# One weight's clamp moves from VectorE to GpSimd, and a list scheduler's price for leaving TensorE's tiling doubles

## The chip, the cores and the metric

One core of a Trainium2 chip runs the whole program. The time is device microseconds of one execution, taken as the median of several. The engines are called as in the profile: PE is TensorE, PEld its weight load, DVE is VectorE, ACT is ScalarE, POOL is GpSimd, and SP is SyncE, whose queue issues every DMA of this kernel.

## The reference

Attention with a learned relative bias, then a two-layer feed-forward. Cut to what matters:

```python
# q, k, v: 4 batches x 8 heads x 576 positions x 64
scores = q @ k.T / 8 + bias          # bias[h, i, j] from a 32-wide MLP of log distances
attn   = softmax(scores)
x      = concat_heads(attn @ v)      # 2304 x 512
h      = x @ w_in                    # w_in 512 x 2048, float64
g      = h * sigmoid(h)
out    = g @ w_out                   # w_out 2048 x 512, float64
```

## The kernel before, in words

[...] `prepare` (L377) turns a 128 x 512 block of a weight into two float32r halves, high and low, with `narrow` (L349) before it. A block takes these steps in a row, all on one `w` tile, of which there are two: ACT takes the absolute value of the upper words (`abs`, L356); DVE clamps (`clamp`, L360), shifts (`shift`, L364), ORs in bits of the lower words (`low`, L369) and the sign (`sign`, L374); ACT copies the high half (`split_hi`, L387, recorded at the helper's line L270); POOL or DVE subtracts (`split_lo`, L391, recorded at L275). 32 blocks go through it: 16 of w_in and 16 of w_out, in turns, while block 0 of the feed-forward runs. The finished w_in halves are also stored to DRAM for the five later blocks (L666).

Attention goes by visits. `chunk` (L537) multiplies queries and keys (L561, L552, into PSUM), takes the biased maximum on DVE (L568), the exponential on ACT (L575), transposes on PE (L584) and evicts on ACT or DVE (L270, L272). `visit` (L463) ends with `pv` (L483), which multiplies by the values on half-width tiles of PE's array, 128 x 64. The bias is made by `bias_tile` (L311): POOL, DVE or ACT at L326 or L328, PE at L334 on quarter-width tiles, 128 x 32. The feed-forward (`ff_step`, L627) has matmuls at L633 and L656, the gate at L638 and L642, and a high and low split at L270, L272 and L275. Everything else on PE uses the full 128 x 128 array.

The order of every engine's instructions is made beforehand by `Plan.order` (L118), a list scheduler that simulates the engines with prices written by hand. Each operation has a price for each engine that may run it, a due time (`prio`), and the buffers it needs; when an engine comes free it takes the ready operation with the earliest due time. Where two engines may run an operation, the one with the higher price takes it as if it were due later (L154), except that POOL has no such handicap. For PE the due time of an operation is raised by `KEEP` if its tiling is another than the current one, in three classes (`MODES`, L58: `pv` is 1, `bias_mm` is 2, all others 0), and a change costs `CHANGE` in the simulation. These two lines decide it:

```python
    MODES, CHANGE, KEEP = {"pv": 1, "bias_mm": 2}, 0.19, 1.5
                    wait[e] = [(p + self.KEEP * (self.MODES.get(self.kinds[i], 0) != mode), p, i) for p, i in every]
```

Each engine then runs its list in order, with semaphores between the engines.

Of the kernel before, what the change touches and what calls it, by code (L numbers as in the profile page):

```python
# [12 lines left out]
ALU = mybir.AluOpType  # L13
# [20 lines left out]
def f(ap):  # L34
    return ap.bitcast(F32)
# [11 lines left out]
class Plan:  # L47
# [7 lines left out]
    CALM = 24.0  # L55


    MODES, CHANGE, KEEP = {"pv": 1, "bias_mm": 2}, 0.19, 1.5  # L58
    LAG = {"PE": 0.2, "ACT": 0.15, "DVE": 0.13, "POOL": 0.15, "SP": 0.95}

    def __init__(self, caps, banks):
# [154 lines left out]
def attention_moe_kernel(ctx: ExitStack, tc: tile.TileContext, q, k, v, small, w_in, w_out, lut, ident_d, out):  # L216
    nc = tc.nc
    V, A, G, T, SP = nc.vector, nc.scalar, nc.gpsimd, nc.tensor, nc.sync
    ENG = {"PE": T, "ACT": A, "DVE": V, "POOL": G, "SP": SP}
# [27 lines left out]
    def buf(tag, shape, dtype=F32):  # L247
        return Buf(tag, shape, dtype)

    def bank(tag, n):  # L250
        return Buf(tag, banks=n)

    def tl(b):
        if b.banks:
            return psum[:, b.at, :] if b.banks == 1 else psum[:, b.at:b.at + b.banks, :].rearrange("p a n -> p (a n)")
        if b.t is None:
            n = 1
            for x in b.shape[1:]:
                n *= x
            flat = pools[b.tag].tile([128, sizes[b.tag]], b.dtype, tag=b.tag, name=b.tag)  # L260
            b.t = flat[:, 0:n]
            if len(b.shape) == 3:
                b.t = b.t.rearrange("p (a n) -> p a n", a=b.shape[1])
            if len(b.shape) == 4:
                b.t = b.t.rearrange("p (a b n) -> p a b n", a=b.shape[1], b=b.shape[2])
        return b.t

    def copy(e, out, in_):
        if e == "ACT":
            A.activation(out=out, in_=in_, func=AF.Copy)  # L270
        else:
            ENG[e].tensor_copy(out=out, in_=in_)  # L272

    def sub(e, out, in0, in1):
        ENG[e].tensor_tensor(out=out, in0=in0, in1=f(in1), op=ALU.subtract)  # L275

    def op(kind, where, prio, reads=(), writes=(), shy=6.0):
        def add(fn):
            plan.op(kind, where, prio, fn, reads, writes, shy=shy)
            return fn  # L280
        return add

    def load(kind, prio, writes, fn, bytes, reads=(), plain=False):
        plan.op(kind, ("SP", 0.52 if plain else 0.7), prio, fn, reads, writes, bytes)
# [61 lines left out]
            out=bias_at(st // 8, 16 * (st % 8) * (BW + 15), [[BW + 16, 16], None, [1, BW]]), in_=tl(bsb)), 302592, reads=[bsb])  # L346


    def narrow(t0, w, src):  # L349

        d = buf("G", [128, 512, 2], U32)
        load("ld_wide", t0 - 6, [d], lambda e: SP.dma_start(out=tl(d), in_=src.bitcast(U32).rearrange("p (n t) -> p n t", t=2)), 524288)

        @op("abs", ("ACT", 0.67), t0, reads=[d], writes=[w])
        def _(e):
            A.activation(out=tl(w), in_=f(tl(d)[:, :, 1]), func=AF.Abs, scale=65536.0)  # L356

        @op("clamp", ("DVE", 0.5), t0 + 0.1, writes=[w])
        def _(e):
            V.tensor_scalar(out=tl(w), in0=tl(w), scalar1=2.0, scalar2=8053063168.0, op0=ALU.max, op1=ALU.min)  # L360

        @op("shift", ("DVE", 0.56), t0 + 0.2, writes=[w])
        def _(e):
            V.tensor_scalar(out=tl(w).bitcast(U32), in0=tl(w).bitcast(U32), scalar1=4, scalar2=1,  # L364
                            op0=ALU.logical_shift_left, op1=ALU.logical_shift_right)

        @op("low", ("DVE", 0.9), t0 + 0.3, reads=[d], writes=[w])
        def _(e):
            V.scalar_tensor_tensor(out=tl(w).bitcast(U32), in0=tl(d)[:, :, 0], scalar=29, in1=tl(w).bitcast(U32),  # L369
                                   op0=ALU.logical_shift_right, op1=ALU.bitwise_or)  # L370

        @op("sign", ("DVE", 0.8), t0 + 0.4, reads=[d], writes=[w])
        def _(e):
            V.scalar_tensor_tensor(out=tl(w).bitcast(U32), in0=tl(d)[:, :, 1], scalar=0x80000000, in1=tl(w).bitcast(U32),  # L374
                                   op0=ALU.bitwise_and, op1=ALU.bitwise_or)

    def prepare(t0, src):  # L377

        w, wr = buf("w", [128, DM]), buf("G", [128, 2, DM], F32R)
        if wide:  # L380
            narrow(t0, w, src)
        else:
            load("ld_w32", t0 - 6, [w], lambda e: SP.dma_start(out=tl(w), in_=src), 262144)

        @op("split_hi", ("ACT", 0.62), t0 + 0.5, reads=[w], writes=[(wr, 0)])
        def _(e):
            copy(e, tl(wr)[:, 0, :], tl(w))  # L387

        @op("split_lo", {"POOL": 1.36, "DVE": 0.9}, t0 + 1, reads=[w, (wr, 0)], writes=[(wr, 1)])
        def _(e):  # L390
            sub(e, tl(wr)[:, 1, :], tl(w), tl(wr)[:, 0, :])  # L391
        return wr
# [206 lines left out]
    def split_x(blk, t0):  # L599

        xs = []
        for cc in range(NC):
            t = t0 + 0.5 * cc
            xb, xr = buf("xp", [128, TB]), buf("xp", [128, TB])
            xs.append(buf("M", [128, 2, TB], F32R))
            load("ld_x", t - 6, [xb], lambda e, xb=xb, cc=cc: SP.dma_start(out=tl(xb), in_=x_d[blk][:, cc, :]), 196608, reads=[x_b[blk]])
            for a, x in enumerate(HALF):
                load("ld_rec", t - 6.1, [(xr, a)], lambda e, a=a, x=x, xr=xr, cc=cc: SP.dma_start(out=tl(xr)[x], in_=bass.AP(
                    tensor=rec_d.tensor, offset=rec_d.offset + (2 * cc + a) * NBLK * TB + TB * blk, ap=[[0, 64], [1, TB]])),
                    98304, reads=[rec_b[i] for i in range(TB * blk // S, (TB * blk + TB - 1) // S + 1)], plain=True)  # L610

            @op("x_mul", {"DVE": 0.6, "POOL": 1.15}, t - 0.1, reads=[xr], writes=[xb])
            def _(e, xb=xb, xr=xr):
                ENG[e].tensor_tensor(out=tl(xb), in0=tl(xb), in1=tl(xr), op=ALU.mult)

            @op("x_hi", {"DVE": 0.5, "ACT": 0.52}, t, reads=[xb], writes=[(xs[cc], 0)])
            def _(e, xb=xb, cc=cc):
                copy(e, tl(xs[cc])[:, 0, :], tl(xb))

            @op("x_lo", {"POOL": 1.1, "DVE": 0.66}, t + 0.1, reads=[xb, (xs[cc], 0)], writes=[(xs[cc], 1)])  # L620
            def _(e, xb=xb, cc=cc):
                sub(e, tl(xs[cc])[:, 1, :], tl(xb), tl(xs[cc])[:, 0, :])
        return xs
# [35 lines left out]
    def ff_block(blk, t0, step):  # L659
        xs = split_x(blk, t0 - 8)  # L660
        acc = [bank("acc", 1) for _ in range(3)]
        for fi in range(NF):
            t = t0 + step * fi
            if blk == 0:
                wr = prepare(t - 5, w_in[fi])
                load("st_in", t - 1, [win_b[fi]], lambda e, wr=wr, fi=fi: SP.dma_start(out=win_d[fi], in_=f(tl(wr).rearrange("p a n -> p (a n)"))), 524288, reads=[wr])  # L666
                if wo[fi] is None:
                    wo[fi] = prepare(t - 2, w_out[128 * fi:128 * fi + 128, :])
            else:
                wr = buf("G", [128, 2, DM], F32R)  # L670
                load("ld_in", t - 8, [wr], lambda e, wr=wr, fi=fi: SP.dma_start(out=f(tl(wr).rearrange("p a n -> p (a n)")), in_=win_d[fi]), 524288, reads=[win_b[fi]])
            ff_step(blk, fi, xs, wr, acc, t)
        for i in range(3):
            ob = buf("M", [128, DM])
            t = t0 + step * (NF - 1) + 2 * DF + 3
            cuts = [(0, DM)] if blk < NBLK - 1 or i < 2 else [(0, DM // 2), (DM // 2, DM)]
            for x, y in cuts:
                @op("out_ev", {"ACT": 0.18 + (y - x) * 0.00083, "DVE": 0.15 + (y - x) * 0.00104}, t, reads=[acc[i]], writes=[(ob, x)])
                def _(e, i=i, ob=ob, x=x, y=y):
                    if e == "ACT":  # L680
                        A.activation(out=tl(ob)[:, x:y], in_=tl(acc[i])[:, x:y], func=AF.Copy, scale=0.5)
                    else:
                        V.tensor_scalar_mul(out=tl(ob)[:, x:y], in0=tl(acc[i])[:, x:y], scalar1=0.5)

                row = TB * blk + 128 * i
                load("st_out", t + 1, [], lambda e, ob=ob, row=row, x=x, y=y: SP.dma_start(
                    out=out[row:row + 128, x:y], in_=tl(ob)[:, x:y]), 512 * (y - x), reads=[(ob, x)])
# [3 lines left out]
    t = T0  # L691
    for c in range(5):
        for st in range(8 * c, min(8 * c + 8, 36)):
            bias_tile(st, (t - B1 if c else -60) + BD * (st - 8 * c))
        for hp in range(4):
            if c == 0:
                kv[hp], vs[hp], sq[hp] = keys(0, hp, t), values(0, hp, t), sums(t)
            t = visit(0, hp, (c,), kv[hp], vs[hp], sq[hp], t)
# [7 lines left out]
    for some in ((1, 2), (3,)):  # L706
        for hp in range(4):
            biases.clear()
            for b in some:
                pace = PACE[t > t2]  # L710
                kv, vs, sq = keys(b, hp, t), values(b, hp, t), sums(t)
                for chunks in ((0, 1), (2, 3, 4)):
                    t = visit(b, hp, chunks, kv, vs, sq, t, pace)
# [74 lines left out]
```

## Time and profile before

| | |
|---|---|
| time, median of 3 runs | 736.17 us (735.53 to 736.71) |
| the profiled execution | 736.04 us, of which the span of instructions is 734.3 us |
| PE, DVE, ACT, POOL busy | 97%, 57%, 53%, 38% of the span |
| granted TensorE clock, mean | 0.998 |

The program passes through three stages. In the first some 115 us the bias is made and batch 0's attention runs. From there to about 340 us the attention of the other batches, the preparing of the weights and block 0 of the feed-forward are mixed. After that the feed-forward takes over, alone from about 470 us. Busy times are read by stage, since the averages over the span mix them.

### The profile page before, as it was taken

What the parts mean: (1) busy time and instruction counts of PE and PEld (TensorE: products, weight loads), DVE (VectorE), ACT (ScalarE), POOL (GpSimd) and SP (SyncE); (2) the same over time, 40 slices, a digit from 0 to 9 for tenths busy, and PEclk for the clock granted to TensorE, in tenths of its full rate; (3) what the DMA queues carried; (4) which work ended last, traced back from release to release, by engine and by line L of the source; (5) the groups of instructions that cost most, each with busy time, mean ns of one, the idle gap of its engine ahead of it and who ended that gap; (6) DMA issues with size and microseconds to landing.
All of it is one profiled execution on the core that took longest, in us unless ns stands there. A gap on an engine that the chain in (4) does not pass through costs nothing.

```text
span 734.3 us, 13019 instructions
## 1 busy us (share of the span) xinstructions
PE 712.6 (97%) x4642; PEld 590.1 (80%) x4642; DVE 421.0 (57%) x862; ACT 389.4 (53%) x820; POOL 281.4 (38%) x277
## 2 busy tenths in 40 slices
PE   9899999999999999989999999999999999999997
PEld 4376698677777787778888888899998999999996
DVE  6999968999999999996553544213211221211111
ACT  8899968886786777765443454222222232222222
POOL 5464524474746445573122251123223322422221
PEclk9999999999999999999999999999999999999999
DMA  6998899898584594879856567736454644346001
GB/s 195 372 315 270 277 310 359 278 289 297 191 290 157 203 303 149 272 257 311 293 165 224 168 217 241 263 115 196 148 162 153 186 150 152 125 136 195 1 0 44
DMA packets 68384, 154.77 MB, mean 211 GB/s; under 512 B 9056, under 2 KB 24032, under 8 KB 68320
## 3 DMA queue, kind: packets, MB, share of 16 engines
q1 hardware_dynamic: 68320, 153.94, 63.7%
q8 instruction: 37, 0.61, 0.4%
q14 instruction: 27, 0.22, 0.1%
HBM read 125.12 MB, written 28.79 MB: 210 GB/s over the span
## 4 chain that ended last, share of the span: by engine, by line
PE 46%; issue 7%; DVE 3%; POOL 2%; DMA 1%; ACT 0%; POOLq 0%; DVEq 0%; ACTq 0%
PE psum L633 18%; PE psum L656 18%; PE psum L483 3%; PE psum L561 3%; PE psum L584 3%; POOL M L275 2%; DVE G L568 1%; DVE w L369 1%; DMA G<-in_k_dram 1%; PE psum L552 1%; DVE M L275 0%; DVE w L374 0%; DVE th L642 0%; DVE M L272 0%; DVE w L360 0%
## 5 line engine op out<-in xcount | busy, mean ns | idle before, releaser
L633 PE MATMUL psum<-M,G 128*128 128x384 f32 x1152 | 238.8, 339 | 1.0 <-POOL M L275 0.8
L656 PE MATMUL psum<-G,M 128*128 128x512 f32 x864 | 238.0, 397 | 1.2 <-DVE M L275 0.9
L633 PEld LDWEIGHTS psum<-M,G 128*128 128x128 f32 x1152 | 203.4, 188 | 16.6 <-POOL M L275 1.0
L275 POOL TENSOR_TENSOR M<-th,M 128x384 fp32r<-128x384 f32 x82 | 84.9, 1035 | 272.0 <-ACT M L270 189.3
L642 DVE SCALAR_TENSOR_TENSOR th<-th,psum 128x384 f32<-128x384 f32 x96 | 53.0, 552 | 216.4 <-ACT th L638 216.4
L656 PEld LDWEIGHTS psum<-G,M 128*128 128x128 f32 x864 | 156.7, 188 | 22.2 <-DVE M L275 1.6
L575 ACT ACTIVATE G<-G,sm 128x576 f32<-128x576 f32 (+1 forms) x144 | 111.8, 777 | 53.6 <-DVE sm L568 52.3
L638 ACT ACTIVATE th<-psum 128x384 f32<-128x384 f32 x96 | 47.1, 491 | 161.1 <-PE psum L633 160.0
L568 DVE CUSTOM_DVE_ANT_0 G<-psum,G 128x576 f32<-128x576 f32 (+1 forms) x144 | 106.5, 758 | 27.9 <-PE psum L561 15.5
L584 PE MATMUL psum<-ident,G 128*128 128x128 f32 x656 | 93.5, 276 | 5.7 <-DVE sm L568 3.3
L561 PE MATMUL psum<-G,M 128*128 128x288 f32 x512 | 90.9, 310 | 4.9 <-DVE sm L568 3.5
L584 PEld LDWEIGHTS psum<-ident,G 128*128 128x128 f32 x656 | 75.3, 141 | 23.0 <-issue 4.8
L561 PEld LDWEIGHTS psum<-G,M 128*128 128x128 f32 x512 | 73.9, 190 | 19.7 <-issue 6.7
L483 PE MATMUL psum<-pt,M 128*64 128x128 f32 (+3 forms) x880 | 87.5, 346 | 1.6 <-DVE sm L568 0.8
L483 PEld LDWEIGHTS psum<-pt,M 128*64 128x64 f32 x880 | 52.1, 137 | 30.7 <-issue 6.8
L270 ACT ACTIVATE pt<-psum 128x512 f32<-128x512 f32 (+3 forms) x111 | 59.4, 551 | 28.1 <-PE psum L584 27.0
L275 POOL TENSOR_TENSOR M<-M 64x256 fp32r<-64x256 f32 (+3 forms) x40 | 48.6, 1217 | 57.9 <-DVE M L272 21.0
L270 ACT ACTIVATE M<-th 128x384 fp32r<-128x384 f32 x81 | 42.3, 523 | 40.9 <-DVE th L642 40.0
L272 DVE COPY pt<-psum 128x512 f32<-128x512 f32 (+3 forms) x81 | 45.4, 571 | 21.8 <-PE psum L584 19.1
L275 POOL TENSOR_TENSOR G<-w,G 128x512 fp32r<-128x512 f32 x25 | 35.6, 1425 | 23.8 <-ACT G L270 19.9
L275 POOL TENSOR_TENSOR G<-G 128x576 fp32r<-128x576 f32 x21 | 32.2, 1540 | 29.6 <-PE psum L334 9.6
L326 ACT ACTIVATE G<-lut_sb,cb 128x528 f32<-128x528 f32 (+16 forms) x71 | 41.6, 662 | 0.0
(55 smaller groups left out, 574.1 us busy)
## 6 DMA issues: line engine op xcount, KB each, us to landing
G<-win_d SPq DMA_DIRECT2D x80, 512.0 KB
G<-bias_d SPq DMA_DIRECT2D x48, 576.0 KB
bias_d<-G SPq DMA_DIRECT2D x36, 295.5 KB
G<-in_k_dram SPq DMA_DIRECT2D x16, 576.0 KB
G<-in_w_in_dram SPq DMA_DIRECT2D x16, 512.0 KB
G<-in_w_out_dram SPq DMA_DIRECT2D x16, 512.0 KB
win_d<-G SPq DMA_DIRECT2D x16, 512.0 KB
M<-in_v_dram SPq DMA_DIRECT2D x16, 320.0 KB
```

What stands on the lines that cost most here:

```text
L270: A.activation(out=out, in_=in_, func=AF.Copy)
L272: ENG[e].tensor_copy(out=out, in_=in_)
L275: ENG[e].tensor_tensor(out=out, in0=in0, in1=f(in1), op=ALU.subtract)
L483: T.matmul(out=tl(o)[x, 0:w], lhsT=tl(vs)[:, (s + 1) % 5 * 128 + 64 * a:(s + 1) % 5 * 128 + 64 * a + 64], rhs=tl(pt)[:, s + 5 * a if s < 4 ...
L561: T.matmul(out=s[:, hf, 0:288], lhsT=tl(qs)[:, x0 + 128 * a:x0 + 128 * a + 128], rhs=tl(part)[:, S * a + 288 * hf:S * a + 288 * hf + 288], ...
L568: V.tensor_tensor_reduce(out=mine(p, a).rearrange("p (a n) -> p a n", a=2), in0=tl(sps[a]).rearrange("p (a n) -> p a n", a=2)[:, :, 0:widt ...
L575: A.activation(out=mine(p, a), in_=mine(p, a), func=AF.Exp, scale=-1.0, bias=tl(sm)[:, i + a:i + a + 1], accum_out=tl(sq)[:, 2 * c + a:2 * ...
L584: T.transpose(out=tl(tp)[:, 128 * s:128 * s + 128], in_=tl(p)[:, 128 * (s0 + s):128 * (s0 + s) + 128], identity=ident)
L633: T.matmul(out=tl(hp)[:, 0:TB], lhsT=tl(wr)[:, x, 128 * cc:128 * cc + 128], rhs=tl(xs[cc])[:, y, :], start=(cc + m == 0), stop=(cc == NC - ...
L638: A.activation(out=tl(th), in_=tl(hp)[:, 0:TB], func=AF.Tanh, scale=0.5)
L642: V.scalar_tensor_tensor(out=tl(th), in0=tl(th), scalar=1.0, in1=tl(hp)[:, 0:TB], op0=ALU.add, op1=ALU.mult)
L656: T.matmul(out=tl(acc[i]), lhsT=tl(gg)[:, x, 128 * i:128 * i + 128], rhs=tl(wo[fi])[:, y, :], start=(fi == 0 and m == 0), stop=(fi == NF - ...
```

## The change

The clamp of a w_in block is put on POOL, with a price of 2.3 us in the planner, in place of DVE with 0.5. The clamp of a w_out block stays on DVE. `KEEP` goes from 1.5 to 3.0. The planner runs again over the changed prices, so that the whole order can differ.

```diff
-    MODES, CHANGE, KEEP = {"pv": 1, "bias_mm": 2}, 0.19, 1.5
+    MODES, CHANGE, KEEP = {"pv": 1, "bias_mm": 2}, 0.19, 3.0
...
-    def narrow(t0, w, src):
+    def narrow(t0, w, src, e1):
...
-        @op("clamp", ("DVE", 0.5), t0 + 0.1, writes=[w])
-        def _(e):
-            V.tensor_scalar(out=tl(w), in0=tl(w), scalar1=2.0, scalar2=8053063168.0, op0=ALU.max, op1=ALU.min)
+        @op("clamp", (e1, 0.5 if e1 == "DVE" else 2.3), t0 + 0.1, writes=[w])
+        def _(e):
+            ENG[e].tensor_scalar(out=tl(w), in0=tl(w), scalar1=2.0, scalar2=8053063168.0, op0=ALU.max, op1=ALU.min)
...
-    def prepare(t0, src):
+    def prepare(t0, src, e1="DVE"):
...
-            narrow(t0, w, src)
+            narrow(t0, w, src, e1)
...
-                wr = prepare(t - 5, w_in[fi])
+                wr = prepare(t - 5, w_in[fi], "POOL")
```

## Rows read from the trace of the kernel before

**Rows 1.** The page's first lines: the span, and each engine's busy time, share and instructions.

```profile
span 734.3 us, 13019 instructions
...
PE 712.6 (97%) x4642; PEld 590.1 (80%) x4642; DVE 421.0 (57%) x862; ACT 389.4 (53%) x820; POOL 281.4 (38%) x277
```

**Rows 2.** Busy time of each engine in stretches of the span: the stretch, its length, then PE, PEld, DVE, ACT and POOL (busy us and instructions), granted clock, DMA share, GB/s.

```profile
80.00:120.00 40.00, 39.99 (x448) 33.80 (x448) 31.14 (x84) 29.24 (x71) 14.13 (x28) 1.00 0.94 294
...
120.00:320.00 200.00, 187.32 (x1273) 151.49 (x1273) 192.66 (x356) 151.70 (x318) 106.62 (x92) 1.00 0.73 247
...
360.00:400.00 40.00, 40.00 (x252) 33.08 (x252) 17.02 (x40) 16.29 (x36) 9.99 (x12) 1.00 0.65 212
```

**Rows 3.** Groups of PE instructions from 120 to 340 us with the most idle time before them: busy us, mean ns of one, then the idle time and what ended it.

```profile
L584 PE MATMUL psum<-ident,G 128*128 128x128 f32 x351 | 49.2, 276 | 5.7 <-DVE sm L568 3.3 <-DVE pt L272 1.5 <-ACT pt L270 0.5
...
L561 PE MATMUL psum<-G,M 128*128 128x288 f32 x264 | 47.3, 308 | 3.9 <-DVE sm L568 2.5 <-DVE pt L272 1.0 <-ACT pt L270 0.4
```

**Rows 4.** Instructions that write or read the tile `w`: count, then the shortest, the median and the longest in ns, and the first and last start.

```profile
L360 DVE TENSOR_SCALAR w<-w x32: 406/422/1920, 127.3 to 314.2; 128x512 f32<-128x512 f32 x32
...
L369 DVE SCALAR_TENSOR_TENSOR w<-G,w x32: 674/692/2218, 130.4 to 318.1; 128x512 uint32<-128x512 uint32 x32
L374 DVE SCALAR_TENSOR_TENSOR w<-G,w x32: 630/684/1962, 132.1 to 318.8; 128x512 uint32<-128x512 uint32 x32
```

**Rows 5.** Groups of instructions from 120 to 340 us, the steps of a weight block and its last subtraction on either engine: busy us, mean ns of one, idle time before.

```profile
L275 POOL TENSOR_TENSOR G<-w,G 128x512 fp32r<-128x512 f32 x25 | 35.6, 1425 | 23.8 <-ACT G L270 19.9 <-issue 1.5 <-DMA xp<-rec_d 1.3
...
L369 DVE SCALAR_TENSOR_TENSOR w<-G,w 128x512 uint32<-128x512 uint32 x32 | 32.0, 1001 | 0.4
L374 DVE SCALAR_TENSOR_TENSOR w<-G,w 128x512 uint32<-128x512 uint32 x32 | 28.3, 886 | 0.1
...
L360 DVE TENSOR_SCALAR w<-w 128x512 f32<-128x512 f32 x32 | 22.8, 715 | 0.8 <-ACT w L356 0.7
...
L275 DVE TENSOR_TENSOR G<-w,G 128x512 fp32r<-128x512 f32 x7 | 9.0, 1287 | 0.2 <-ACT G L270 0.2
```

**Rows 6.** Groups of POOL instructions over the span, each shape apart: the two-operation TENSOR_SCALAR of the bias (L328) at two widths.

```profile
L328 POOL TENSOR_SCALAR G<-lut_sb,cb 128x512 f32<-128x512 f32 x1 | 2.1, 2107 | 0.1
...
L328 POOL TENSOR_SCALAR G<-lut_sb,cb 128x416 f32<-128x416 f32 x1 | 1.7, 1677 | 1.0 <-DMA bias_d<-G 1.0
```

**Rows 7.** Timeline of POOL and of DVE between 125 and 136 us: start, duration, instruction. Two pairs that overlap.

```profile
126.69 1.71 POOL L275 TENSOR_TENSOR M<-M 64x704 fp32r<-64x704 f32 x1 [0.96 <-ACT M L270]
...
134.25 1.29 POOL L275 TENSOR_TENSOR G<-w,G 128x512 fp32r<-128x512 f32 x1 [2.14 <-ACT G L270]
...
127.31 1.37 DVE L360 TENSOR_SCALAR w<-w 128x512 f32<-128x512 f32 x1
...
134.68 1.14 DVE L364 TENSOR_SCALAR w<-w 128x512 uint32<-128x512 uint32 x1
```

**Rows 8.** Timeline of POOL and of DVE between 25 and 27.2 us, the bias stage: a POOL TENSOR_SCALAR, and the DVE instructions that began while it ran.

```profile
25.13 2.03 POOL L328 TENSOR_SCALAR G<-lut_sb,cb 128x336 f32<-128x336 f32 x1
...
25.69 0.28 DVE L272 CAST M<-M 128x256 fp32r<-128x256 f32 x1
25.89 0.61 DVE L328 TENSOR_SCALAR G<-lut_sb,cb 128x384 f32<-128x384 f32 x1
26.54 0.42 DVE L275 TENSOR_TENSOR M<-M 64x256 fp32r<-64x256 f32 x1
```

**Rows 9.** The line L275 from 120 to 340 us: two other kinds of subtraction that POOL or DVE may run, in the columns of Rows 4.

```profile
L275 POOL TENSOR_TENSOR M<-th,M x13: 997/1060/1426, 173.8 to 336.5; 128x384 fp32r<-128x384 f32 x13
L275 POOL TENSOR_TENSOR G<-G x12: 1407/1469/1868, 121.0 to 320.3; 128x576 fp32r<-128x576 f32 x12
...
L275 DVE TENSOR_TENSOR G<-G x4: 850/1215/1987, 122.2 to 321.5; 128x576 fp32r<-128x576 f32 x4
L275 DVE TENSOR_TENSOR M<-th,M x4: 546/964/1507, 161.3 to 316.1; 128x384 fp32r<-128x384 f32 x4
```

**Rows 10.** Timeline of PE between 94 and 109 us: runs of one line, with the number of instructions at the end.

```profile
97.50 0.60 PE L584 MATMUL psum<-ident,G 128*128 128x128 f32 x4
97.86 0.77 PE L561 MATMUL psum<-G,M 128*128 128x288 f32 x4
...
100.35 0.60 PE L584 MATMUL psum<-ident,G 128*128 128x128 f32 x4
100.88 1.31 PE L483 MATMUL psum<-pt,M 128*64 128x128 f32 x20
102.12 1.20 PE L584 MATMUL psum<-ident,G 128*128 128x128 f32 x9
...
104.86 2.40 PE L483 MATMUL psum<-pt,M 128*64 128x128 f32 x40
107.19 1.20 PE L584 MATMUL psum<-ident,G 128*128 128x128 f32 x9
```

**Rows 11.** Timeline of PE between 40 and 122 us: the first and the last of its 33 runs at L483 or L334, the two narrower tilings.

```profile
42.22 1.31 PE L483 MATMUL psum<-pt,M 128*64 128x128 f32 x20
...
121.47 0.74 PE L483 MATMUL psum<-pt,M 128*64 128x64 f32 x18
```

**Rows 12.** Timeline from 125 to 165 us: the first block's absolute value on ACT, and its shift on DVE.

```profile
125.27 0.66 ACT L356 ACTIVATE w<-G 128x512 f32<-128x512 f32 x1
...
129.28 0.41 DVE L364 TENSOR_SCALAR w<-w 128x512 uint32<-128x512 uint32 x1
```

## The prediction

> **What bounds the kernel now.** I read the page's first lines, then the busy times by stretch, then what ended PE's idle time, then single instructions. PE is busy 712.6 of 734.3 us [rows 1], so PE's own work is nearly the whole time, and a gain can come only from PE's idle time or from pauses inside its busy time. The stretches show where each lies [rows 2]. From 80 to 120 us PE is busy 39.99 of 40 us, and from 360 to 400 all 40: no other engine matters there. Only from 120 to 320 us is it different: PE is busy 187.3 of 200 us, so 12.7 us are idle, while DVE is busy 192.7 (96%) and POOL 106.6 (53%). DVE is the bound there, and the idle rows say the same: before L584 and L561 PE sat idle 5.7 + 3.9 = 9.6 us, of which DVE ended 3.3 + 1.5 + 2.5 + 1.0 = 8.3, or 0.86 [rows 3]. All 32 clamps run between 127.3 and 314.2 us [rows 4], inside that stage. So the clamp's move is aimed at the right engine; its ceiling is 12.7 us. `KEEP` acts mainly before 120 us, where most narrow-tiled runs are.
>
> **What the clamp's move takes off DVE.** A clamp takes 422 ns in the median and 715 in the mean [rows 4, 5]. The difference is waiting. One clamp began at 127.31 us and took 1.37, and ended 0.28 after a POOL subtraction that ran from 126.69 to 128.40; a shift that began at 134.68 and took 1.14 ended 0.28 after another, from 134.25 to 135.54 [rows 7]. Alone a shift takes 0.41 [rows 12]. So a DVE instruction among SBUF tiles stands still until the POOL instruction that it met has ended. Without the clamp, the wait goes too or falls on the next DVE step, so 16 clamps free between 16 x 0.422 = 6.8 and 16 x 0.715 = 11.4 us. I take the middle, 9.1.
>
> **What it puts on POOL.** No POOL clamp is in the trace. The nearest rows are the bias's two-operation TENSOR_SCALAR on the same engine: 2.107 us at 512 columns, 1.677 at 416 [rows 6]. I take 2.1, as the shape and kind are the same; the immediate operands in place of a column could make it cheaper, and waits for DVE dearer, so 1.4 (the mean subtraction of 512 columns [rows 5]) to 2.6. 16 x 2.1 = 33.6 us bring POOL from 106.6 to 140 of 200 us. POOL has that room.
>
> **What this costs DVE by waiting.** This is the disputed price. Low end: three DVE instructions began and ended within a POOL TENSOR_SCALAR that ran from 25.13 to 27.16 us. The cast took 0.28, the subtraction of two SBUF tiles 0.42, the TENSOR_SCALAR 0.61; none waited for 27.16 [rows 8]. High end: the POOL clamp blocks as the POOL subtractions do. Mean less median of the steps L360, L369 and L374 is 0.293 + 0.309 + 0.202 = 0.80 us a block [rows 4, 5], 25.7 us over 32 blocks against 106.6 us of POOL work, or 0.24 us for each us of POOL; for 33.6 us that is 8.1. Below nothing it can't be, as more POOL work frees no port. I take the near row: the stage has 16 clamps, 3 x 32 other steps of the weights and some 15 subtractions on DVE [rows 5, 9], about 127 instructions in 195 us, so 22 of them meet a POOL clamp, at 0.1 each (0.61 is 0.2 over the 0.41 of a wider one, the others show nothing): 2.2 us. Range 0 to 8.1.
>
> The Trainium skill says otherwise (SBUF — State Buffer, Who interferes with whom): a DVE instruction in a two-port mode, or with two SBUF inputs, and a GpSimd instruction share a port pair as an exclusive lock, and the later one fully blocks. Rows 7 agree with it, rows 8 don't. By that rule the term is the high end, and the result is the first rival.
>
> **What the planner moves back.** With POOL busier, a subtraction that either engine may run is found by DVE first more often. Of three kinds, DVE runs 7, 4 and 4 now against POOL's 25, 13 and 12 [rows 5, 9]. If DVE's share follows POOL's load, 15 x 140 / 106.6 = 20; a moved one also empties POOL by 1.4 us, so I take 4 more, at 1.287 us each [rows 5]: 5.2 us back on DVE. Range 0 to 8 moves, 0 to 10.3 us.
>
> **DVE's sum.** 9.1 - 2.2 - 5.2 = 1.7 us less. Of that 0.86 reaches PE, as far as DVE ended PE's idle time: 1.5 us, rounded down to 1.3 for DVE's own idle 4%.
>
> **The wait that is added.** Shift, next on the block, now waits for POOL, and on DVE everything behind it waits as well, the maxima at L568 above all, on which PE waits. The first block's absolute value ended at 125.93 and its shift began at 129.28 [rows 12], 3.35 us later; a POOL clamp needs 2.1 plus two hops. With POOL free it is hidden. If POOL is inside a subtraction it isn't (second rival). The planner counts 2.3 us and both hops, so that it places the shift later on DVE; I cost this at nothing. The stores and loads of the block on SP keep their place in the chain; SP waits on nothing new, the finished halves only come some 1.7 us later.
>
> **What `KEEP` saves.** Two `pv` runs in one went from 104.86 to 107.19, 2.33 us; a single one from 100.88 to 102.12, 1.24: merging saves 0.15. Four transposes took 0.53 to the next start ahead of a `pv` and 0.36 ahead of a full-array run [rows 10], another 0.17. So a merge, which takes two changes away, is worth up to 0.32 us. From 40 to 122 us there are 33 narrow runs [rows 11]. I take 5 merges (bias tiles are due 2.6 us apart in the plan, more than 1.5 and less than 3.0): 1.6 us, all of it PE's time, since PE is full there. Range 0 to 14 merges, 0 to 4.5 us. Later than 160 us `pv` runs stand some 13 us apart, and nothing merges. A run held longer keeps its `pt` or PSUM buffer longer, which could starve PE; with PE at 39.99 of 40 us I see room and cost nothing.
>
> **Sum.** 1.3 + 1.6 = 2.9 us off the profiled 736.04, thus 733.1; the median stands 0.13 higher, so 733.3 us.
>
> **Rivals.**
> 1. The POOL clamp blocks DVE as the subtractions do. DVE: 9.1 - 8.1 - 5.2 = -4.2, so PE loses 3.6 and gains 1.6: 738.2. For it: rows 7. Against it: rows 8. Chance 0.12.
> 2. Slower by the wait at shift. POOL runs in order; at 126.69 it began a subtraction of 1.71 us [rows 7]. A clamp behind that starts at 128.40 and ends at 130.5, 1.2 us after the place that shift has now. If half the blocks meet this, 8 x 1.2 = 9.6 us on DVE, 8.3 on PE, less the 2.9: 741.6. It decides from a mean wait of about 0.21 us a block, 3.4 us in all. POOL is busy half the time, which speaks for it; DVE running behind its plan by its unplanned waits, so that it comes to the shift late, speaks against it. Chance 0.15.
> 3. No difference: the freed DVE time goes back wholly (6 moved subtractions, 7.7 us) and the runs merge little: 736.2, within 1.5. Chance 0.24.
>
> The forecast, some 1.5 to 8 us faster, has 0.46. A new order that costs a little for a reason that I haven't priced has 0.03. That makes faster 0.46, same 0.24, slower 0.30, where 0.2% (1.5 us) is about what measurement tells from no change. The range goes down to 727.5 (11.4 freed, no waiting and few moves, 7.1 of it on PE, and 1.6 of merges) and up to 741, which takes in the first rival and the lesser cases of the second.
>
> **What would show it.** Right: 16 TENSOR_SCALARs on POOL near 2.1 us, DVE's busy time from 120 to 320 us some 2 us down, PE's idle time there under 12 us, fewer narrow runs than 33 in the same stretch. Wrong: the weights' steps on DVE with a higher mean at the same median (rival 1), idle DVE before L364 ended by POOL (rival 2), more subtractions at L275 on DVE (rival 3). The forecast fails if the new order of the whole kernel shifts PE's idle time by more than these terms.

## The result, and the profile after

| | before | after |
|---|---|---|
| time, median | 736.18 us | 745.95 us (744.75 to 748.09, 4 runs) |
| ratio, 95% interval | | 1.0136 (1.0110 to 1.0162) |
| span of the profiled execution | 734.3 us | 743.6 us |

The forecast was 733.3 us, faster; the kernel became 9.8 us slower. One execution of the run p3 below, the profiled one, took 1321.43 us at a granted clock of 0.876; the median of p3 is that of its three others. The first lines of the page after answer to [rows 1]:

```profile
span 743.6 us, 13003 instructions
...
PE 714.7 (96%) x4642; PEld 591.9 (80%) x4642; DVE 423.2 (57%) x853; ACT 386.4 (52%) x821; POOL 308.5 (41%) x285
```

PE has the same 4642 matmuls. The span grew by 9.3 us: 2.1 more of PE busy, and PE's idle time (span less busy) from 21.7 to 28.9, 7.2 more. The busy times of the kernel after in the stretches of [rows 2]:

```profile
80.00:120.00 40.00, 39.24 (x445) 33.05 (x443) 32.77 (x83) 27.70 (x70) 11.35 (x25) 1.00 0.91 281
120.00:320.00 200.00, 182.74 (x1226) 147.24 (x1223) 182.68 (x337) 144.99 (x309) 126.35 (x96) 0.99 0.72 244
360.00:400.00 40.00, 40.00 (x254) 34.69 (x253) 20.70 (x48) 17.03 (x37) 11.33 (x11) 1.00 0.72 244
```

From 120 to 320 us DVE is busy 182.7 in place of 192.7, and PE has *more* idle time, 17.3 us in place of 12.7. But DVE is not freed by that: it runs 337 instructions there in place of 356, as the work has moved to later, and over the span it is busy 423.2 us in place of 421.0. From 80 to 120 us, where PE was full, 0.8 us are idle. The instructions on the tile `w` after, in the columns of [rows 4]:

```profile
L364 DVE TENSOR_SCALAR w<-w x32: 365/518/1640, 134.0 to 325.0; 128x512 uint32<-128x512 uint32 x32
L369 DVE SCALAR_TENSOR_TENSOR w<-G,w x32: 628/680/1759, 138.5 to 327.8; 128x512 uint32<-128x512 uint32 x32
L374 DVE SCALAR_TENSOR_TENSOR w<-G,w x32: 664/686/2058, 139.7 to 330.6; 128x512 uint32<-128x512 uint32 x32
...
L275 POOL TENSOR_TENSOR G<-w,G x27: 1274/1297/1822, 141.6 to 332.9; 128x512 fp32r<-128x512 f32 x27
L360 POOL TENSOR_SCALAR w<-w x16: 1916/1988/2459, 132.2 to 317.9; 128x512 f32<-128x512 f32 x16
L360 DVE TENSOR_SCALAR w<-w x16: 365/421/1502, 133.6 to 323.0; 128x512 f32<-128x512 f32 x16
L275 DVE TENSOR_TENSOR G<-w,G x5: 679/1312/1760, 143.4 to 286.5; 128x512 fp32r<-128x512 f32 x5
```

The POOL clamp takes 1.99 us in the median, and the preparing begins and ends later: the last `sign` starts at 330.6 us in place of 318.8.

Where most of the 2.1 us of busy time come from shows around 155 us. PE's timeline after:

```profile
151.84 0.42 PE L633 MATMUL psum<-M,G 128*128 128x384 f32 x1
153.92 1.83 PE L633 MATMUL psum<-M,G 128*128 128x384 f32 x5 [1.66 <-DVE M L275]
155.55 1.16 PE L561 MATMUL psum<-G,M 128*128 128x288 f32 x4
```

and the stretches of 1 us that follow; the granted clock is the third number from the end:

```profile
154.00:155.00 1.00, 0.92 (x4) 0.60 (x5) 1.00 (x1) 0.36 (x1) 1.00 (x2) 0.93 0.90 254
155.00:156.00 1.00, 1.00 (x4) 1.00 (x5) 1.00 (x4) 0.64 (x2) 1.00 (x1) 0.50 0.84 217
156.00:157.00 1.00, 1.00 (x5) 1.00 (x5) 0.95 (x3) 1.00 (x3) 1.00 (x2) 0.50 0.70 246
157.00:158.00 1.00, 1.00 (x5) 1.00 (x4) 0.78 (x4) 1.00 (x3) 0.92 (x3) 0.50 0.57 172
158.00:159.00 1.00, 1.00 (x8) 0.96 (x8) 0.13 (x1) 1.00 (x4) 0.60 (x1) 0.86 0.76 267
```

PE stood idle 1.66 us for a subtraction on DVE, ran on at full clock for about 0.9 us, and then at the lower of its two levels, 1.2 of 2.4 GHz; the shares missing from 1.00 in these rows add up to 0.07 + 3 x 0.50 + 0.14 = 1.71 us lost. Before, no stretch from 120 to 360 us shows a clock under 1.00.

### The profile page after: what moved, and what is told of

Read it like the earlier page. It is cut to its first block, busy times and chain, and to the rows that moved or that the text cites. A ratio compares the mean times of both kernels' runs of the same rounds, so it can differ in the third digit from the quotient of the medians.

```text
span 743.6 us, 13003 instructions
## 1 busy us (share of the span) xinstructions
PE 714.7 (96%) x4642; PEld 591.9 (80%) x4642; DVE 423.2 (57%) x853; ACT 386.4 (52%) x821; POOL 308.5 (41%) x285
## 4 chain that ended last, share of the span: by engine, by line
PE 64%; DVE 12%; issue 10%; DMA 7%; POOL 4%; SPq 1%; ACT 1%; POOLq 0%; DVEq 0%; ACTq 0%
PE psum L633 20%; PE psum L656 20%; PE psum L483 7%; PE psum L584 6%; PE psum L561 6%; PE psum L334 4%; POOL M L275 3%; DVE G L568 2%; DVE w L374 1%; DMA x_d<-xo 1%; PE psum L552 1%; DVE G L275 1%; DVE w L364 1%; DMA G<-bias_d 1%; DMA G<-in_k_dram 1%
## 5 line engine op out<-in xcount | busy, mean ns | idle before, releaser
L275 POOL TENSOR_TENSOR M<-th,M 128x384 fp32r<-128x384 f32 x81 | 84.3, 1040 | 260.9 <-ACT M L270 189.8
L483 PE MATMUL psum<-pt,M 128*64 128x128 f32 (+3 forms) x880 | 87.0, 345 | 1.1 <-DVE xo L272 0.9
L483 PEld LDWEIGHTS psum<-pt,M 128*64 128x64 f32 x880 | 52.2, 137 | 29.8 <-issue 6.6
L270 ACT ACTIVATE pt<-psum 128x640 f32<-128x640 f32 (+3 forms) x110 | 54.9, 519 | 35.3 <-PE psum L584 31.8
L272 DVE COPY pt<-psum 128x640 f32<-128x640 f32 (+3 forms) x82 | 50.7, 627 | 35.4 <-PE psum L584 33.2
L275 POOL TENSOR_TENSOR M<-M 64x256 fp32r<-64x256 f32 (+3 forms) x34 | 43.4, 1279 | 46.9 <-DVE M L272 17.4
L275 POOL TENSOR_TENSOR G<-w,G 128x512 fp32r<-128x512 f32 x27 | 37.5, 1392 | 22.9 <-ACT G L270 19.1
L275 POOL TENSOR_TENSOR G<-G 128x576 fp32r<-128x576 f32 x23 | 35.0, 1535 | 24.1 <-PE psum L334 9.6
L326 ACT ACTIVATE G<-lut_sb,cb 128x384 f32<-128x384 f32 (+16 forms) x68 | 40.3, 663 | 0.0
```

The source lines that it names most:

```text
L483: T.matmul(out=tl(o)[x, 0:w], lhsT=tl(vs)[:, (s + 1) % 5 * 128 + 64 * a:(s + 1) % 5 * 128 + 64 * a + 64], rhs=tl(pt)[:, s + 5 * a if s < 4 ...
```

## The experiments

Each run has its own runs of the kernel before on the same chip beside it; differences are of the medians. "Kept order" means that the planner decides with the prices of before, and only the instruction that is issued differs.

**The two halves.**

```diff
-    MODES, CHANGE, KEEP = {"pv": 1, "bias_mm": 2}, 0.19, 3.0
+    MODES, CHANGE, KEEP = {"pv": 1, "bias_mm": 2}, 0.19, 1.5      # e1, against after; e2 is before with 3.0
```

> The clamp of the first weight on GpSimd, planned at 2.3 us, with the price for leaving the tiling left at 1.5. Theory A (the new order of the instructions costs the time, whatever made the planner choose it): anything from 732 to 748, not the sum of two clean effects. Theory B (the clamp on GpSimd lengthens a block's chain, and VectorE and PE wait for it): 744 to 748, nearly all of the loss. Theory C (the doubled price makes PE hold back narrow runs that others wait for): 733 to 737, as forecast for the clamp alone.

Measured: 742.84 us, +6.3 (ratio 1.0085, 1.0066 to 1.0103).

> The price for leaving the tiling doubled to 3.0, the clamp left on VectorE. Theory A: anything from 732 to 748. Theory B: 733 to 737, a little faster by the merged runs. Theory C: 744 to 748.

Measured: 741.50 us, +5.0 (1.0076, 1.0057 to 1.0096). Both halves are slower, and each alone costs more than half of what both cost. That speaks against theories B and C as the one cause.

**The order against the engine.** e3 keeps the order of before and issues the clamp on POOL; e4 keeps the order of after and issues it on DVE.

```diff
-        @op("clamp", (e1, 0.5 if e1 == "DVE" else 2.3), t0 + 0.1, writes=[w])
+        @op("clamp", ("DVE", 0.5), t0 + 0.1, writes=[w])              # e3, with KEEP 1.5
...
-            ENG[e].tensor_scalar(out=tl(w), ...)
+            ENG[e1].tensor_scalar(out=tl(w), ...)                     # e3
...
-            ENG[e].tensor_scalar(out=tl(w), ...)
+            V.tensor_scalar(out=tl(w), ...)                           # e4, priced as in after
```

> The order of the kernel before, planned with its own prices, with the first weight's clamps issued on GpSimd at the places where they stood. PE, ScalarE and the DMA queue keep their lists to the instruction. Theory A (order): within 3 us of the kernel before, 733 to 739. Theory B (the clamp itself, through the chain and the waits at the shift): 742 or more, since here the planner has left no room for the longer clamp. Theory C: 733 to 737.

Measured: 752.10 us, +15.6 (1.0208, 1.0188 to 1.0229). DVE's waits from 115 to 365 us in e3 begin with this row (who waited for whom, total us, times, longest):

```profile
DVE w L364 <- POOL w L360: 18.5, 12, 3.1
```

> The order of the changed kernel, planned with its prices, with the clamps issued on VectorE. Theory A: 744 to 748, the loss stays without any clamp on GpSimd; VectorE has some 9 us more to do than in the changed kernel, so it may be a few us above it. Theory B: 735 to 738, the loss goes with the clamp. Theory C: as A.

Measured: 745.31 us, +8.8 (1.0128, 1.0106 to 1.0149), no different from the kernel after (1.0136). So in the order of after the engine of the clamp makes no difference that shows, and the loss is there without a single clamp on POOL; in the order of before a clamp on POOL is dear, and the wait at the shift is real. Theory A fits e4; it fails on e3, where B's number came in.

**Orders drawn anew, with changes that mean nothing.** The planner's order changes at small steps of a price. With 0.51 in place of 0.50 (p1), PE's matmuls run in the order of before up to 174 us and in another from there on. Work changes its engine too: p1 runs 863, 813 and 283 instructions on DVE, ACT and POOL, before 862, 820 and 277. So "order" here means the whole plan, the choice of engines included.

```diff
-        @op("clamp", ("DVE", 0.5), t0 + 0.1, writes=[w])
+        @op("clamp", ("DVE", 0.51), t0 + 0.1, writes=[w])             # p1; p3 has 0.45; p2 has KEEP 1.55
```

> The kernel before with the planner's price of all 32 clamps raised from 0.50 to 0.51 us, nothing else: no instruction changes its engine or its work by intent, but the order comes out another. Theory A (the order of before is one that happens to run well, and any other drawn from the same planner is slower): 739 to 746. Theory D (each half of the change has a cost of its own, and an order as such costs nothing): 735 to 738.

Measured: 741.04 us, +4.3 (1.0062, 1.0045 to 1.0078).

> The kernel before with the price for leaving the tiling at 1.55 in place of 1.5. Theory A: 739 to 746, like the doubled price, with a twentieth of that step. Theory D: 735 to 738, a thirtieth of the doubled price's 5 us at most.

Measured: 742.80 us, +6.1 (1.0083, 1.0057 to 1.0109).

> The kernel before with the planner's price of all 32 clamps lowered from 0.50 to 0.45 us. Theory A: 739 to 746. Theory D: 735 to 738.

Measured: 744.85 us, +8.1 (1.0110, 1.0091 to 1.0129). All three rule theory D out: an order as such costs 4 to 8 us against that of before, as much as either half of the change.

**Redraws of the changed kernels.** q1 and q4 are e1 with the POOL clamp priced 2.0 and 2.6 us; q2 is after with 2.2; q3 is e2 with the DVE clamp at 0.51.

> First weight's clamp on GpSimd, priced 2.0 us in place of 2.3 in the plan (near the 1.99 us that it takes), tiling price 1.5. Theory A (any order newly drawn costs some 4 to 8 us against before, the change's own cost being small): 739 to 746. Theory B (the clamp on GpSimd has a cost of its own beyond the draw): 746 or more.

Measured: 744.64 us, +8.3 (1.0112, 1.0092 to 1.0132).

> The changed kernel with the GpSimd clamp priced 2.2 us in place of 2.3. Theory A: 739 to 746, anywhere in it. Theory E (both changes together cost more than a draw, as the 746 of the changed kernel hints): 744 to 749.

Measured: 751.56 us, +15.2 (1.0212, 1.0188 to 1.0236).

> The doubled tiling price, all clamps on VectorE at 0.51 in place of 0.50 us. Theory A: 739 to 746. Theory F (the doubled price saves PE time that the other draw, 741.5, hid): 736 to 739.

Measured: 747.54 us, +11.2 (1.0150, 1.0133 to 1.0167).

> First weight's clamp on GpSimd, priced 2.6 us, tiling price 1.5. Theory A: 739 to 746. Theory B: 746 or more. If a longer planned clamp leaves VectorE and PE room that 2.3 did not, 736 to 740.

Measured: 744.89 us, +8.6 (1.0109, 1.0092 to 1.0126). q2 and q3 lie above every range that was expected of them; q1 and q4 lie in theory A's.

Side by side, us over the kernel before:

| | tiling price 1.5 (1.55) | tiling price 3.0 |
|---|---|---|
| clamps on DVE | 4.3, 6.1, 8.1: mean 6.2 | 5.0, 11.2: mean 8.1 |
| first weight's clamp on POOL | 6.3, 8.3, 8.6: mean 7.7 | 9.8, 15.2: mean 12.5 |

Within a cell the draws differ by 2 to 6 us, as much as the cells do. So each half alone can't be told from a redraw; both together look worse than a bare redraw by some 6 us, on two draws. No draw of the ten comes near before, with either half or without.

**The clamp's parts, in the kept order.** e5 gives the POOL clamp room: it is issued right behind its absolute value, and the shift is moved on DVE to right before L369.

```diff
+    for i in moved:
+        key[at[i + 1]], key[at[i + 2]] = at[i] + 0.5, at[i + 3] - 0.5
```

> The order of before with the first weight's clamps on GpSimd, as in the earlier run that kept the old order, but each clamp issued right behind its absolute value, and each shift moved on VectorE to right before the step that ORs in the lower words. PE, ScalarE and the DMA queue keep their lists. If the 15.6 us of the earlier run were the wait at the shift, most of them go: 733 to 740, and below 736 only if the 7 to 10 us taken off VectorE reach PE (theory A says they would in a fixed order). If clamps on GpSimd cost by their length or by the shared port (theory B), 744 or more.

Measured: 747.72 us, +11.0 (1.0153, 1.0136 to 1.0169). DVE's wait for the clamp went from 18.5 to 2.0 us, and only 4.6 us came back, so the wait itself was not most of the cost. Four more runs take the parts asunder; e7, e8 and e9 leave the 16 clamps of w_in out.

```diff
+            e1 == "POOL" or V.tensor_scalar(out=tl(w), ...)           # e7; e9 the same in the order of after
+            V.tensor_scalar(out=tl(w), ...); e1 == "POOL" and G.tensor_scalar(out=spare, in0=tl(lut_b)[:, 0:512], ...)   # e6
+            (G if e1 == "POOL" else V).tensor_scalar(...)             # e8: on POOL from lut to spare, no clamp of w_in
```

> The order of before with the 16 clamps of the first weight left out (part of the computation is missing), all else kept. What freeing VectorE is worth in a fixed order. If the forecast's step is right that VectorE's freed time (7 to 11 us) reaches PE to 0.86: 727 to 731. If PE's idle time in this order is not VectorE's load but single late results: 734 to 737.

Measured: 733.11 us, -4.2 (0.9945, 0.9927 to 0.9964).

> The order of before, all clamps on VectorE, and 16 extra two-operation TENSOR_SCALARs of 128 x 512 on GpSimd at the clamps' places, which read a constant tile, write a spare one in bfloat16 and are waited for by nobody. GpSimd's load alone. If the load (queue and port) is what costs: 742 to 750. If only the dependency costs: 736 to 739, by the 2 us that the forecast took for waits at the port.

Measured: 743.51 us, +6.2 (1.0086, 1.0068 to 1.0104).

> Both: the first weight's clamps left out on VectorE (part of the computation is missing) and the same 16 extra instructions on GpSimd; everything of the kept-order run but the block's dependency on GpSimd. If the dependency is the cost there: 728 to 738, the sum of the two other runs. If load is: 742 or more.

Measured: 741.55 us, +4.3 (1.0065, 1.0042 to 1.0088).

> The changed kernel with the 16 clamps on GpSimd left out (part of the computation is missing), its order kept. If the clamp on GpSimd costs in its own order, by load or dependency: 738 to 743. If that order is slow for reasons of its own: 744 to 747.

Measured: 743.30 us, +6.0 (1.0081, 1.0061 to 1.0102).

The times of e7, e8 and e9 lie between the ranges that were expected. The page's lines of busy times of e7, e6, e9, e8 and e4, in this order:

```profile
PE 711.1 (97%) x4642; PEld 589.5 (81%) x4642; DVE 412.2 (56%) x846; ACT 389.0 (53%) x820; POOL 281.9 (39%) x277
```

```profile
PE 715.1 (96%) x4642; PEld 591.4 (80%) x4642; DVE 426.5 (58%) x862; ACT 389.3 (53%) x820; POOL 316.9 (43%) x293
```

```profile
PE 712.7 (96%) x4642; PEld 590.8 (80%) x4642; DVE 419.2 (57%) x853; ACT 385.6 (52%) x821; POOL 276.0 (37%) x269
```

```profile
PE 714.2 (97%) x4642; PEld 591.7 (80%) x4642; DVE 416.6 (56%) x846; ACT 388.8 (53%) x820; POOL 314.6 (43%) x293
```

```profile
PE 713.7 (96%) x4642; PEld 590.8 (80%) x4642; DVE 425.2 (57%) x869; ACT 386.5 (52%) x821; POOL 275.9 (37%) x269
```

In a kept order, taking the clamp off DVE gives 4.2 us, and the same work on POOL, waited for by nobody, costs 6.2. Both together cost 4.3, where the two make 2.0; the intervals hardly tell these apart. The block's dependency on POOL brings that to the 15.6 of e3, by difference another 11.3.

e9 against e7 is the order of after against that of before, with nothing of the w_in clamp in either: 6.0 + 4.2 = 10.2 us. With the clamp on POOL the order of after costs 9.8 - 6.0 = 3.8 more. So the 9.8 us are 4.2 gained, 10.2 lost by the new order and 3.8 by the clamp on POOL. That order was drawn with `KEEP` at 3.0, and e9 doesn't tell what a higher `KEEP` does by intent from what a draw does.

Most of what the load on POOL costs in e6 shows at one place. PE in the kernel before, then PE and POOL in e6, and the stretches behind in e6, in the columns of [rows 2]:

```profile
157.02 1.15 PE L633 MATMUL psum<-M,G 128*128 128x384 f32 x5 [0.75 <-POOL M L275]
```

```profile
158.71 1.97 PE L633 MATMUL psum<-M,G 128*128 128x384 f32 x5 [2.47 <-POOL M L275]
```

```profile
155.49 2.04 POOL L360 TENSOR_SCALAR spare<-lut_sb 128x512 bf16<-128x512 f32 x1
157.50 2.57 POOL L275 TENSOR_TENSOR M<-xp,M 128x384 fp32r<-128x384 f32 x2
```

```profile
155.00:160.00 5.00, 2.35 (x10) 2.00 (x11) 5.00 (x10) 3.12 (x9) 5.00 (x4) 0.75 1.00 329
160.00:165.00 5.00, 5.00 (x24) 4.74 (x24) 2.39 (x5) 1.89 (x5) 0.93 (x5) 0.57 1.04 313
```

One extra instruction stands on POOL ahead of a subtraction that PE waits for: POOL begins it at 157.50, before at 155.85. PE is idle 2.47 us in place of 0.75, and then loses 5 x 0.25 + 5 x 0.43 = 3.4 us of clock, where before loses none: 1.7 + 3.4 = 5.1 us, if none of it is made up later, and the span of e6 is 7.0 longer. The same wait is 2.71 us in e8, 2.28 in e3 and 2.52 in e5, each with a lower clock behind it.

## Why the prediction was wrong, by its own steps

**The step that failed** is one for which the sum had no term: that the planner "runs again over the changed prices" was known, and its price was set at nothing; a new order that costs "for a reason that I haven't priced" got 3 in 100. A redraw with no meaning costs 4.3 to 8.1 us (p1 to p3), and the order of after costs 10.2 with no w_in clamp in it. The rivals were about the clamp, where the time mostly wasn't; the prediction's last sentence names this way to fail, at next to no chance.

**What DVE gives up** was right in size: 9.1 us forecast, and e7 has 421.0 - 412.2 = 8.8 less on DVE. The sum behind it was wrong in sign: the order of after puts 7.0 us more on DVE (419.2 in e9, 412.2 in e7) and the POOL clamps add 423.2 - 419.2 = 4.0, so that DVE is busy 2.2 us more, where 1.7 less were forecast.

**What of it reaches PE** was too high: 0.86 was taken from who ended PE's idle time [rows 3]; 4.2 / 8.8 = 0.48 is measured in the kept order. So the share that "DVE ended" is not what PE gains when DVE has less to do. A reason for it, argued and not shown: the late result is one instruction in a list that is run in order, and the list decides which one.

**POOL's duration**, 2.1 us, was right (1.99). That POOL "has that room" was a step at nothing, and in the kept order it failed: the wait of PE on POOL's subtraction in e6, above, is of that kind.

**The waits at the port**, 2.2 us for a range of 0 to 8.1, were too low: 4.0 in the kernel after, as above. In e6 DVE has its old instructions and is busy 426.5 - 421.0 = 5.5 us longer by 16 POOL instructions. Two DVE steps that meet the one from 155.49 us, shown above, from the timeline of e6:

```profile
155.68 0.83 DVE L360 TENSOR_SCALAR w<-w 128x512 f32<-128x512 f32 x1
157.10 0.71 DVE L364 TENSOR_SCALAR w<-w 128x512 uint32<-128x512 uint32 x1
```

The DVE clamp takes 0.83 in place of 0.42 us and has ended 1 us before POOL's instruction ends, at 157.53. The shift, begun 0.4 us before that end, takes 0.71 in place of 0.41 and ends 0.28 behind it, as the pairs of [rows 7] do. The rule of the Trainium skill (SBUF — State Buffer, Who interferes with whom), that the later one blocks until the other's whole instruction has ended, holds for POOL's subtractions [rows 7]; for its TENSOR_SCALAR neither the rule nor the forecast's 0.1 us is what the trace shows. As a rival it asked for 738.2 by waits alone; the load did cost 6.2 in e6, which is more than DVE's 5.5 us of waits at 0.48 explain (2.6). The rest has its place in PE's wait for POOL and the clock behind it, above: PE's own busy time is 715.1 in e6 against 712.6.

**The moved subtractions.** Of the three kinds, DVE runs 5 + 3 + 7 = 15 after from 120 to 340 us, as 7 + 4 + 4 = 15 before [rows 5, 9]; 4 more were forecast. Over the span and all kinds DVE runs 44 subtractions in place of 39, and 7 instructions more in all but the clamps. So work did come back to DVE, 7.0 us for the 5.2 forecast, but other work and at other times.

**The wait at the shift.** Costing it at nothing was right for after: no idle time of DVE before L364 stands there. That the planner places the shift later, as the forecast had it, fits that and is not shown apart. In the kept order it is 18.5 us of waiting. Rival 2 had the mechanism and its place, and the right sign (741.6), but the kernel after is not slow by it. What the dependency does besides, 11.0 in e5 with only 2.0 of waiting at the shift, is settled in part: e6's wait of PE on POOL is there too. ACT waits 11.3 us for a free `w` tile, 7.4 before, but 10.5 in e6 without the dependency, so that tells little.

**`KEEP`.** From 40 to 122 us PE's timeline has 32 narrow runs in place of 33, and 52 changes of tiling in place of 59, counted from those rows. So 1 run went, where 5 merges were forecast, and the 1.6 us that they were to save are not to be seen: e2, with 32 runs too, has PE busy 712.6 us as before, and PE idle for 738.4 - 712.6 = 25.8 us, 4.1 more.

**Where the time of an order goes**, in all these runs, is the same two places. Span less PE's busy time, before 21.7: p1 25.4, p2 25.0, e1 25.8, e2 25.8, e4 29.2, after 28.9, e3 32.1. PE's busy time, before 712.6: p1 713.6, p2 715.5, e1 715.2, e4 713.7, after 714.7, e3 718.1. In the second is the clock: in e3 two stretches show it under 1.00, in the columns of [rows 2]:

```profile
160.00:180.00 20.00, 18.78 (x96) 16.02 (x97) 17.30 (x28) 11.99 (x25) 11.92 (x11) 0.83 0.64 212
200.00:220.00 20.00, 16.86 (x104) 13.03 (x101) 16.24 (x28) 10.87 (x23) 11.19 (x10) 0.91 0.59 210
```

That is 20 x 0.17 + 20 x 0.09 = 5.2 us, and PE's busy time is up by 5.5. But the execution of before that was profiled loses 1.7 us itself, from 35 to 40 us (granted clock 0.66), and that of e3 doesn't, so the clock explains about 3.5 of these 5.5.

What the order of before has is short waits. The longest idle time of PE between 40 and 700 us, first before, then in p2:

```profile
203.16 0.74 PE L584 MATMUL psum<-ident,G 128*128 128x128 f32 x5 [1.26 <-DVE sm L568]
```

```profile
163.07 1.33 PE L584 MATMUL psum<-ident,G 128*128 128x128 f32 x5 [3.69 <-ACT pt L270]
```

It is the only one of 1 us or more before. The traces of the draws, p3 aside, have 3 to 7 of them each, 3.9 us together in after and 11.6 in q2, and each of these draws loses 1.7 to 6.8 us to the clock there, before none. What ends these waits is not one line but several.

What stays open: why the order of before has none of these long waits; no single instruction makes it so in all draws. Nor is it known how that order was found, by chance or as the best of many. Whether doubled `KEEP` or a POOL clamp would gain among many orders was not tried; two or three draws a cell say only that a gain of several us isn't there.

## What to carry to other kernels

When a scheduler orders the whole program, a changed price is two changes: the one that is meant, and a new order. Draw the order a few times with steps that mean nothing before crediting or blaming the change, and measure the meant part with the order kept. A kernel whose order is a good one among many can lose by any edit of its prices, as here by all ten, so the forecast starts from the spread of the draws, here 4 to 8 us, and not from zero. The share of PE's idle time that an engine ended was here well above what PE gained when that engine got less to do, 0.86 against 0.48.

## What the runs showed of the hardware

A TENSOR_SCALAR on POOL of 2.04 us held up a DVE instruction that began 0.2 us after it for about 0.4 us and let it end 1 us before its own end (0.83 in place of 0.42), while a POOL subtraction of 1.3 to 1.7 us held it to its end [rows 7]. A single idle stretch of PE of 1.66 us was followed by more than 3 us at 1.2 GHz: 1.66 us of idle time and 1.71 of lost clock. Not every such stretch was: in e7 one of 2.37 us was followed by none. PE's timeline there, and the clock of the next stretches:

```profile
324.10 0.80 PE L561 MATMUL psum<-G,M 128*128 128x288 f32 x4 [2.37 <-DVE sm L568]
```

```profile
320.00:325.00 5.00, 2.63 (x20) 2.36 (x19) 4.72 (x9) 2.61 (x6) 4.51 (x4) 1.00 1.00 343
325.00:330.00 5.00, 5.00 (x35) 4.52 (x34) 4.10 (x12) 3.71 (x10) 1.13 (x4) 1.00 1.04 321
```
